# Numerators and denominators of a compressive memory in one product of 136 columns, copied by ScalarE, and an output that ends in halves

## The chip, the cores and the metric

The kernel runs on one core of one Trainium2 chip. The metric is the device time of one execution, in microseconds (us). The core has a matrix engine (TensorE, PE in the profile; its weight loads are PEld), three engines for elementwise work (VectorE or DVE, ScalarE or ACT, GpSimd or POOL), a queue for transfers (SyncE or SP) and two on-chip memories: SBUF, and the eight banks of PSUM that matmuls write.

## The reference

Two branches work on the same 2048 rows of 512 numbers, and a gate mixes them row by row: `out = g * a + (1 - g) * b`.

- `b` is a gated feed-forward layer of width 1792: `gelu(x @ w_gate) * (x @ w_up) @ w_down`.
- `a` is attention with 32 heads of 16 numbers, in 4 segments of 512 rows, with a memory that runs from segment to segment. What matters here:

```python
for s in range(N):
    p = softmax(qs @ ks.T * scale + mask)
    a_dot = p @ vs
    num = einsum('bhld,bhde->bhle', phi(qs), M)
    den = einsum('bhld,bhd->bhl', phi(qs), z)[..., None] + 1e-06
    o = gb * (num / den) + (1.0 - gb) * a_dot      # gb = sigmoid(beta), one per head
    M = M + einsum('bhld,bhle->bhde', phi(ks), vs)
    z = z + sum_l phi(ks)
a = concat(o) @ wo
```

Segment 0 has an empty memory, so the memory part is computed in segments 1 to 3. Inputs and outputs are bf16.

## The kernel before

**Tiles.** The 32 heads are four chunks `c` of eight heads, so there are 16 pairs (segment, chunk), numbered `i = 4*s + c`. A chunk's queries are 128 partitions (8 heads x 16) by 512 rows. Weights stay in SBUF all the time.

**Attention.** The kernel runs 72 visits. A visit computes a block of logits for four heads at a time into the only tile `lg` of four banks (`group_qk`, line 649, called QK below), ScalarE takes its exp into `pT` (line 654) and GpSimd masks the diagonal (line 658). When a chunk has all its eight blocks, two visits later a "lump" multiplies them with the values (`pv`, line 674, called PV below) into two banks `od`. VectorE transposes these (`oq`, line 681), divides by the softmax sums and scales (`norm`, lines 686 and 687, once for each of two halves), transposes the result into the chunk's part of `oT` (`back`, line 692), and adds the memory part `mT` (`add_mem`, line 695). These come 1, 2, 3 and 4 visits after the lump.

**Memory.** After each of the first three segments, `memory` (line 556) adds its products to `Macc`. `u_mask` makes two operands from it for the next segment: `Mn`, block-diagonal by heads with 128 columns a chunk, and `Mz` with 8 columns a chunk. `u_den` multiplies `phi(q)` (tile `pq`) with `Mz` (tile `zd`, line 599), and VectorE adds 1e-6, inverts and multiplies by the head's gate (`rdm`, lines 606, 609, 610), for two chunks at a time. `mem_num` multiplies `pq` with `Mn` into one bank `mn` (line 628); VectorE scales the bank by `rdm` into `tm` (line 632), and SyncE transposes `tm` into `mT` by a transfer (line 640). The scaling and the transfer are issued in `mem_num` itself.

**The other work.** Matmuls of all other parts (K, Q, V, gate, up, down, out) are units of 4 to 16 matmuls in streams: `gT` (line 473), `uT` (494), `dT` (510, 14 matmuls a unit) and `aT` (532, 4 a unit). They write the four banks of the pool `gen` in turn, which `mn`, `zd` and `od` use too. Their results are read out by VectorE, or by ScalarE where `cast` finds room (lines 309 and 313).

**The order.** All engines' instructions are put in order by a planner in the kernel's own Python. `t_pe` and `t_act` are its clocks for TensorE and ScalarE, `passed(pe, dve)` and `act(t)` advance them, `backlog` is VectorE's. Each visit issues QK, then a lump if one is due, then everything due in this visit (`later(n, f)` puts `f` into the n-th visit from now), then fills TensorE with units up to a `goal` at which the next QK may come; the numerator (`mem_num`) asked for at the end of the visit before is issued between two such fills. In the last segment the goal keeps 7.6 us of units (`TAIL_FILL`), and the last four `aT` units, for after the visits. There the last lump and all that is still due are issued:

```python
fill_to(t_pe[0] + TAIL_FILL * 0.42)
for f in pending:
    f()
for _, i in lumps:
    lump(i)
while due:
    for f in due.pop(min(due)):
        f()
fill_to(1e9)
```

`mem_num` of the last chunk runs in visit 72, the last. `left()` sums the units that have not begun. Each engine executes its instructions in the order of issue. `u_out` (lines 522 to 548) multiplies `oT` with `wo`, mixes with the other branch (line 538) and sends 128 rows out (line 547); the last 128 rows go in two halves.

Of the kernel before, what the change touches and what calls it, by code (L numbers as in the profile page):

```python
# [53 lines left out]
def kernel(  # L54
# [44 lines left out]
    gh = const([P, H], F32, "gh")  # L99
    og = const([P, H], F32, "og")  # L100
    Macc = const([P, NC8, 2, 17], F32, "Macc")
    Mn = [const([P, NC8, 128], BF, f"Mn{i}") for i in range(2)]
    Mz = [const([P, NC8, 8], BF, f"Mz{i}") for i in range(2)]
    rdm = [const([P, KT, H], F32, f"rdm{i}") for i in range(2)]
    ktb = const([P, NC8, L], BF, "ktb")
    pk = const([P, KT, D], BF, "pk")
    G = [const([P, HS, L], BF, f"G{i}") for i in range(NG)]
# [90 lines left out]
    def setup_consts():  # L198
        nc.gpsimd.memset(bm[:, :, :], 1.0)
        nc.gpsimd.affine_select(out=bm[:, :, :], in_=bm[:, :, :], pattern=[[-16, 8], [0, 17]],  # L200
                                compare_op=ALU.is_ge, fill=0.0, base=0, channel_multiplier=1)
        nc.gpsimd.affine_select(out=bm[:, :, :], in_=bm[:, :, :], pattern=[[16, 8], [0, 17]],
                                compare_op=ALU.is_ge, fill=0.0, base=15, channel_multiplier=-1)
        nc.vector.tensor_reduce(out=eo[:, 0:1], in_=bm[:, 0:8:2, 16],
                                axis=mybir.AxisListType.X, op=ALU.add)
        nc.vector.tensor_reduce(out=eo[:, 1:2], in_=bm[:, 1:8:2, 16],
                                axis=mybir.AxisListType.X, op=ALU.add)
        for i in range(2):
            ones = V[i][:, :, 0:2 * VE].rearrange("q k (h e) -> q k h e", h=H)[:, :, :, 16:18]
# [312 lines left out]
    def u_out(s, qt):  # L522
        def f():
            oT = oTs[s]
            q0 = s * L + qt * P
            tB = tBs[(s, qt // 2)]
            parts = 2 if (s, qt) == (NSEG - 1, KT - 1) and not general_now[0] else 1
            w = D // parts
            for d0 in range(0, D, w):
                T = gen("aT")  # L530
                for fc in range(FC):
                    nc.tensor.matmul(T[:, 0:w], lhsT=oT[:, fc, qt * P:(qt + 1) * P],  # L532
                                     rhs=wo[:, fc, d0:d0 + w],
                                     start=(fc == 0), stop=(fc == FC - 1))
                    if fc < FC - 1:
                        yield MM512 / parts
                osb = tB[:, qt % 2, d0:d0 + w]
                nc.vector.scalar_tensor_tensor(out=osb, in0=T[:, 0:w],  # L538
                                               scalar=gct[:, s, qt:qt + 1],
                                               in1=osb, op0=ALU.mult, op1=ALU.add)  # L540
                if s == 0 and qt == KT - 2:
                    continue
                if s == 0 and qt == KT - 1:
                    queue[0].dma_start(out2[q0 - P:q0 + P, :].rearrange("(k p) d -> p k d", p=P),
                                       tB[:, :, :])
                else:
                    queue[0].dma_start(out2[q0:q0 + P, d0:d0 + w], osb)
            return MM512
        return 4 * MM512, EVAC, f

# [16 lines left out]
    def u_mask(s):  # L567
        def half(h0):
            for c in (h0, h0 + 1):
                nc.vector.tensor_tensor(  # L570
                    out=Mn[s % 2][:, c, :].rearrange("q (j p d) -> q j p d", j=4, p=2),
                    in0=Macc[:, c, None, :, 0:16].to_broadcast((P, 4, 2, DH)),
                    in1=bm[:, :, 0:16].rearrange("q (j p) d -> q j p d", j=4), op=ALU.mult)
            passed(0.0, 0.6)
            done["Mn", s] = count(("Mn", s)) + 1

        def f():
            nc.vector.tensor_tensor(
                out=Mz[s % 2][:, :, :].rearrange("q c (j p) -> q c j p", j=4),
                in0=Macc[:, :, None, :, 16].to_broadcast((P, NC8, 4, 2)),  # L580
                in1=bm[:, None, :, 16].to_broadcast((P, NC8, 8))
                .rearrange("q c (j p) -> q c j p", j=4), op=ALU.mult)
            if general_now[0]:
                half(0)
                half(2)
            else:
                later(2, lambda: half(0))
                later(8, lambda: half(2))
        return 0.0, 0.2, f

    def u_den(s, pair):
        def f():
            assert general_now[0] or ("q", s, 2 * pair) in ready
            T = gen("zd")
            Tv = T[:, 0:KT * 16].rearrange("p (q h) -> p q h", q=KT)
            for cc in range(2):
                c = 2 * pair + cc
                for qq in range(KT):
                    nc.tensor.matmul(Tv[:, qq, 8 * cc:8 * cc + 8],
                                     lhsT=pq[:, c, qq * P:(qq + 1) * P],  # L600
                                     rhs=Mz[s % 2][:, c, :], start=True, stop=True)
                if cc == 0:
                    yield 0.12
            h0 = 16 * pair
            r = rdm[s % 2][:, :, h0:h0 + 16]
            nc.vector.tensor_scalar_add(r, Tv, 1e-6)

            def f_inv():
                nc.vector.reciprocal(r, r)
                nc.vector.tensor_tensor(out=r, in0=r,  # L610
                                        in1=gh[:, None, h0:h0 + 16].to_broadcast((P, KT, 16)),
                                        op=ALU.mult)
                passed(0.0, 0.8)
                done["inv", s] = count(("inv", s)) + 1
            if general_now[0]:
                f_inv()
            else:
                later(1, f_inv)
            return 0.12
        return 0.24, 0.22, f  # L620

    tms = {}

    def mem_num(s, c):
        assert general_now[0] or (count(("Mn", s)) > c // 2 and count(("inv", s)) > c // 2)
        T = gen("mn")
        for qq in range(KT):
            nc.tensor.matmul(T[:, qq * P:(qq + 1) * P],  # L628
                             lhsT=pq[:, c, qq * P:(qq + 1) * P], rhs=Mn[s % 2][:, c, :],
                             start=True, stop=True)  # L630
        tm = wk2.tile([P, KT, 8, DH], BF, name="tm", tag="tm")
        nc.vector.tensor_tensor(
            out=tm[:, :, :, :], in0=T[:, :].rearrange("p (q h d) -> p q h d", q=KT, h=8),
            in1=rdm[s % 2][:, :, 8 * c:8 * c + 8, None].to_broadcast((P, KT, 8, DH)), op=ALU.mult)
        mT = wk2.tile([P, L], BF, name="mT", tag="mT")
        mTv = mT[:, :].rearrange("p (q t) -> p q t", q=KT)
        if general_now[0]:
            turn(mTv, tm[:, :, :, :].rearrange("p q h d -> p q (h d)"))
        else:
            nc.sync.dma_start_transpose(mTv, tm[:, :, :, :].rearrange("p q h d -> p (q h d)"))  # L640
        tms[(s, c)] = mT

    def group_qk(pieces):
        lg = plg.tile([P, 4, 512], F32, name="lg", tag="lg")
# [236 lines left out]
    us = []  # L881
    for s in range(NSEG - 1):
        us.append(unit(u_mask(s + 1), 0, None, lambda s=s: count(("M", s)) == 1))
        us += [unit(u_den(s + 1, pair), NP * s + 16 + 9 * pair, ("den", s + 1),
                    lambda s=s, pair=pair: ("q", s + 1, 2 * pair) in ready)
               for pair in range(2)]
# [76 lines left out]

    def numerator(s, c):
        room_for_bank()
        mem_num(s, c)
        done["num", s] = count(("num", s)) + 1
        passed(0.3, EVAC)

    def can_num(s, c):  # L970
        if count(("den", s)) <= c // 2 and ("q", s, c - c % 2) in ready:
            need(("den", s), c // 2 + 1)
        return count(("Mn", s)) > c // 2 and count(("inv", s)) > c // 2

    asked = []
    pending = []
# [123 lines left out]
    def general():  # L1100
# [4 lines left out]
        for s in range(NSEG):  # L1105
# [16 lines left out]
            if s > 0:  # L1122
                for c in range(0, NC8, 2):
                    phi_now(pq[:, c:c + 2, :], QT[:, c:c + 2, :])
                run(u_mask(s))
                run(u_den(s, 0))
                run(u_den(s, 1))
# [75 lines left out]
```

## Time and profile before

| what | value |
|---|---|
| median of 3 runs (lowest to highest) | 268.8 us (268.23 to 269.04) |
| the profiled execution's own time | 268.51 us |
| its span in the profile | 266.8 us |
| busy TensorE / VectorE / ScalarE / GpSimd | 261.9 / 200.7 / 209.7 / 155.7 us |
| mean granted TensorE clock | 0.998 |

Rows of the profile name the line of the kernel, the engine, the tile written and the tiles read, and then a count (x8), the busy time and the mean of one instruction in ns, or, in a timeline, the start and the length in us. A releaser in brackets ends the idle time before an instruction. The chain that ended last follows the last instruction back, at each step to what released it.

### The profile page before, as it was taken

To read this page: it belongs to the slowest core of one execution; us is meant where nothing else is said; L and a number is where in the kernel's file an instruction comes from. 1 tells how busy PE (TensorE), PEld (TensorE's weight loads), DVE (VectorE), ACT (ScalarE), POOL (GpSimd) and SP (SyncE) were. 2 spreads that over 40 slices of the span, in tenths; PEclk is the share of its full clock that TensorE was granted. 3 is DMA by queue.
4 is the path that set the end of the run, shared out by engine and by line. 5 is a ranking of instruction groups with operands and counts; after the bars stand their busy time and mean duration, and the time that the engine had idled before them with its cause. 6 is when DMAs were issued, how large, how long until landed. Compare 5 with 4: busy or idle time off the path is not lost.

```text
span 266.8 us, 6876 instructions
## 1 busy us (share of the span) xinstructions
PE 261.9 (98%) x2861; PEld 117.1 (44%) x2861; DVE 200.7 (75%) x394; ACT 209.7 (79%) x164; POOL 155.7 (58%) x298
## 2 busy tenths in 40 slices
PE   7999999999999999999999999999999999999994
PEld 4454434344443444444445344444444444444442
DVE  2899574969569887698887858595978759698364
ACT  4236889988998899889999899889989997657510
POOL 3000158896716979678940899687694099654500
PEclk9999999999999999999999999999999999999999
DMA  6999941200222001300033010401000110003102
GB/s 210 343 168 277 308 121 39 42 4 1 61 64 42 2 0 42 79 6 20 2 61 84 0 23 20 64 20 22 20 23 23 45 22 12 10 20 42 41 22 84
DMA packets 30410, 16.60 MB, mean 62 GB/s; under 512 B 20008, under 2 KB 29096, under 8 KB 30376
## 3 DMA queue, kind: packets, MB, share of 16 engines
q1 hardware_dynamic: 30376, 16.14, 24.8%
q8 instruction: 23, 0.38, 0.6%
q14 instruction: 11, 0.09, 0.1%
HBM read 8.14 MB, written 2.10 MB: 38 GB/s over the span
## 4 chain that ended last, share of the span: by engine, by line
PE 94%; DVE 4%; issue 1%; DVEq 0%
PE dT L510 19%; PE uT L494 18%; PE gT L473 18%; PE lg L649 8%; PE od L674 7%; PE kT L376 5%; PE qT L290 5%; PE aT L532 5%; PE vT L414 4%; PE mn L628 1%; PE warm L166 1%; PE zT L430 1%; DVE G L500 1%; PE MT L556 1%; PE x0T L183 1%
## 5 line engine op out<-in xcount | busy, mean ns | idle before, releaser
L658 POOL TENSOR_SCALAR_AFFINE_SELECT pT<-pT 64x256 bf16<-64x256 bf16 x256 | 112.9, 441 | 94.1 <-ACT pT L654 81.3
L654 ACT ACTIVATE pT<-lg 128x2048 bf16<-128x2048 f32 x72 | 135.1, 1876 | 22.5 <-PE lg L649 21.6
L494 PE MATMUL uT<-x,wup 128*128 128x512 bf16 x224 | 60.6, 380 | 0.0
L473 PE MATMUL gT<-x,wga 128*128 128x512 bf16 x224 | 55.6, 380 | 0.0
L510 PE MATMUL dT<-wdn,G 128*128 128x512 bf16 x224 | 53.9, 380 | 0.0
L500 DVE TENSOR_TENSOR G<-uT,G 128x512 bf16<-128x512 f32 x56 | 38.1, 683 | 6.1 <-PE uT L494 5.9
L386 POOL TENSOR_SCALAR KTm<-ktb,eo 128x512 bf16<-128x512 bf16 x26 | 40.7, 1577 | 1.3
L681 DVE STREAM_TRANSPOSE oq<-od 128x512 f32<-128x512 f32 x32 | 21.0, 695 | 20.1 <-PE od L674 20.1
L473 PEld LDWEIGHTS <-wga 128*128 128x128 bf16 x224 | 20.7, 98 | 24.5 <-issue 2.4
L510 PEld LDWEIGHTS <-G 128*128 128x128 bf16 x224 | 20.4, 98 | 24.3 <-issue 2.8
L494 PEld LDWEIGHTS <-wup 128*128 128x128 bf16 x224 | 20.2, 97 | 24.5 <-issue 4.7
L649 PE MATMUL lg<-QT,KTm 32*128 32x192 bf16 (+7 forms) x512 | 28.6, 287 | 0.0
L313 DVE CAST G<-gT 128x512 bf16<-128x512 f32 x25 | 17.1, 686 | 5.8 <-PE gT L473 5.6
L649 PEld LDWEIGHTS <-KTm 32*128 32x128 bf16 x512 | 8.5, 92 | 29.5 <-issue 29.5
L674 PE MATMUL od<-pT,V 64*32 64x128 bf16 (+7 forms) x512 | 19.3, 284 | 0.0
L674 PE MATMUL od<-pT,Vs 64*32 64x128 bf16 (+7 forms) x512 | 18.9, 284 | 0.1
L488 ACT ACTIVATE G<-G 128x3584 bf16<-128x3584 bf16 x6 | 18.8, 3182 | 0.0
L687 DVE SCALAR_TENSOR_TENSOR o<-oq,ogs,rden 128x256 bf16<-128x256 f32 x32 | 17.1, 535 | 1.1
L376 PE MATMUL kT<-x,wk 128*128 128x512 bf16 x64 | 16.8, 383 | 0.4 <-DVE x L189 0.4
L290 PE MATMUL qT<-x,wq 128*128 128x512 bf16 x64 | 16.6, 379 | 0.0
L538 DVE SCALAR_TENSOR_TENSOR tB<-aT,gct,tB 128x512 bf16<-128x512 f32 (+1 forms) x17 | 11.9, 712 | 5.8 <-PE aT L532 5.5
L532 PE MATMUL aT<-wo,oT 128*128 128x512 bf16 (+1 forms) x68 | 16.2, 367 | 0.0
(96 smaller groups left out, 269.6 us busy)
## 6 DMA issues: line engine op xcount, KB each, us to landing
wup<-in_B_w_up_dram SPq DMA_DIRECT2D x1, 1792.0 KB, 10.4
wdn<-in_B_w_down_dram SPq DMA_DIRECT2D x1, 1792.0 KB
out_dram<-tB SPq DMA_DIRECT2D x13, 128.0 KB, 1.7
wga<-in_B_w_gate_dram SPq DMA_DIRECT2D x1, 1280.0 KB, 10.2
Vs<-V SPq DMA_DIRECT2D x8, 144.0 KB, 3.2
G<-in_A_x_dram SPq DMA_DIRECT2D x2, 256.0 KB, 2.8
wk<-in_A_wk_dram SPq DMA_DIRECT2D x2, 256.0 KB, 4.3
wq<-in_A_wq_dram SPq DMA_DIRECT2D x1, 512.0 KB, 5.7
```

The lines of the kernel that those rows point to most:

```text
L290: nc.tensor.matmul(T[:, :], lhsT=wq[:, fc, c * P:(c + 1) * P], rhs=xS[s % NX][:, fc, :], start=(fc == 0), stop=(fc == FC - 1))
L376: nc.tensor.matmul(T[:, :], lhsT=wk[:, fc, c * P:(c + 1) * P], rhs=xS[s % NX][:, fc, :], start=(fc == 0), stop=(fc == FC - 1))
L386: eng.tensor_scalar(out=KTm[:, (NC8 * s + c) % NK, :, p, :], in0=ktb[:, c, :].rearrange("q (b k) -> q b k", b=NB), scalar1=eo[:, p:p + 1], ...
L473: nc.tensor.matmul(T[:, :], lhsT=wga[:, fc, hs * P:(hs + 1) * P], rhs=xS[s % NX][:, fc, :], start=(fc == 0), stop=(fc == FC - 1))
L494: nc.tensor.matmul(T[:, :], lhsT=wup[:, fc, hs * P:(hs + 1) * P], rhs=xS[s % NX][:, fc, :], start=(fc == 0), stop=(fc == FC - 1))
L500: nc.vector.tensor_tensor(out=g, in0=T[:, :], in1=g, op=ALU.mult)
L510: nc.tensor.matmul(T[:, :], lhsT=G[s % NG][:, hs, qt * P:(qt + 1) * P], rhs=wdn[:, hs, :], start=(hs == 0), stop=(hs == HS - 1))
L532: nc.tensor.matmul(T[:, 0:w], lhsT=oT[:, fc, qt * P:(qt + 1) * P], rhs=wo[:, fc, d0:d0 + w], start=(fc == 0), stop=(fc == FC - 1))
L649: nc.tensor.matmul(lg[:, j, off:off + n], lhsT=KTm[rows, i % NK, b].rearrange("r p k -> r (p k)"), rhs=QT[rows, i % NC8, 64 * b:L], start= ...
L654: nc.scalar.activation(pT[:, :, :], lg[:, :, :], AF.Exp, scale=DH ** -0.5)
L658: nc.gpsimd.affine_select(out=v, in_=v, pattern=[[0, 4], [1, 64]], compare_op=ALU.is_ge, fill=0.0, base=0, channel_multiplier=-1)
L674: nc.tensor.matmul(od[p][32 * j:32 * j + 32, 64 * b:L], lhsT=w[:, 18 * h:18 * h + 32], rhs=t[rows, j, off:off + n], start=(b == 0), stop=( ...
```

## The change

Numerator and denominator come out of one product. `Mn` has 136 columns a chunk, the last 8 of which take the place of `Mz`; the stream units `u_den` go. `mem_num` takes two banks of 272 columns (two blocks of 128 rows each); ScalarE copies each to an f32 tile `raw` in SBUF; the inversion (three VectorE instructions for one chunk) is due one visit later, and the scaling and the transposing transfer two visits later. The planner books 0.9 us on ScalarE for the copies and fills TensorE up to shortly before the end of the visit's exp ahead of the numerator.

The end: the last 256 rows, instead of the last 128, are computed in halves of 256 columns. The rows before the last 128 are still sent in one transfer; the first half of the last rows is sent from ScalarE's queue. At the start, two small reductions become one.

```diff
-    Mn = [const([P, NC8, 128], BF, f"Mn{i}") for i in range(2)]
-    Mz = [const([P, NC8, 8], BF, f"Mz{i}") for i in range(2)]
-    rdm = [const([P, KT, H], F32, f"rdm{i}") for i in range(2)]
+    Mn = [const([P, NC8, 136], BF, f"Mn{i}") for i in range(2)]
...
-        nc.vector.tensor_reduce(out=eo[:, 0:1], in_=bm[:, 0:8:2, 16],
-                                axis=mybir.AxisListType.X, op=ALU.add)
-        nc.vector.tensor_reduce(out=eo[:, 1:2], in_=bm[:, 1:8:2, 16],
+        nc.vector.tensor_reduce(out=eo[:, :],
+                                in_=bm[:, :, 16].rearrange("q (j p) -> q p j", p=2),
                                 axis=mybir.AxisListType.X, op=ALU.add)
...
-            parts = 2 if (s, qt) == (NSEG - 1, KT - 1) and not general_now[0] else 1
+            final = s == NSEG - 1 and not general_now[0]
+            parts = 2 if final and qt >= KT - 2 else 1
...
+                elif final and qt == KT - 2:
+                    if d0 > 0:
+                        queue[0].dma_start(out2[q0:q0 + P, :], tB[:, qt % 2, :])
                 else:
-                    queue[0].dma_start(out2[q0:q0 + P, d0:d0 + w], osb)
+                    q = nc.scalar if final and qt == KT - 1 and d0 == 0 else queue[0]
+                    q.dma_start(out2[q0:q0 + P, d0:d0 + w], osb)
...
-    def u_den(s, pair):
...
     def mem_num(s, c):
+        assert general_now[0] or count(("Mn", s)) > c // 2
+        raw = wk2.tile([P, KT, 136], F32, name="raw", tag="raw", bufs=1)
+        for h in range(2):
+            T = gen("mn")
+            for k in range(2):
+                qq = 2 * h + k
+                nc.tensor.matmul(T[:, 136 * k:136 * k + 136], lhsT=pq[:, c, qq * P:(qq + 1) * P],
+                                 rhs=Mn[s % 2][:, c, :], start=True, stop=True)
+            nc.scalar.copy(raw[:, 2 * h:2 * h + 2, :].rearrange("p k e -> p (k e)"),
+                           T[:, 0:272])
+        rd = wk2.tile([P, KT, 8], F32, name="rd", tag="rd")
+
+        def f_inv():
+            nc.vector.tensor_scalar_add(rd[:, :, :], raw[:, :, 128:136], 1e-6)
+            nc.vector.reciprocal(rd[:, :, :], rd[:, :, :])
+            nc.vector.tensor_tensor(out=rd[:, :, :], in0=rd[:, :, :],
+                                    in1=gh[:, None, 8 * c:8 * c + 8].to_broadcast((P, KT, 8)),
+                                    op=ALU.mult)
+            passed(0.0, 0.3)
+
+        def f_scale():
+            tm = wk2.tile([P, KT, 8, DH], BF, name="tm", tag="tm")
+            nc.vector.tensor_tensor(
+                out=tm[:, :, :, :], in0=raw[:, :, 0:128].rearrange("p q (h d) -> p q h d", h=8),
+                in1=rd[:, :, :, None].to_broadcast((P, KT, 8, DH)), op=ALU.mult)
+            passed(0.0, 0.65)
+            mT = wk2.tile([P, L], BF, name="mT", tag="mT")
...
+                nc.sync.dma_start_transpose(mTv, tm[:, :, :, :].rearrange("p q h d -> p (q h d)"))
+            tms[(s, c)] = mT
...
+        else:
+            act(0.9)
+            later(1, f_inv)
+            later(2, f_scale)
...
     def numerator(s, c):
         room_for_bank()
+        room_for_bank()
         mem_num(s, c)
         done["num", s] = count(("num", s)) + 1
-        passed(0.3, EVAC)
+        passed(0.3)
 
     def can_num(s, c):
-        if count(("den", s)) <= c // 2 and ("q", s, c - c % 2) in ready:
-            need(("den", s), c // 2 + 1)
-        return count(("Mn", s)) > c // 2 and count(("inv", s)) > c // 2
+        return count(("Mn", s)) > c // 2 and ("q", s, c - c % 2) in ready
...
-    act_left[0] = len(visits) * EXP_T + 3 * (GELU_T + 4 * PHI_T)
+    act_left[0] = len(visits) * EXP_T + 3 * (GELU_T + 4 * PHI_T) + 12 * 0.9
...
         fill_to(t_pe[0] + 0.5 * (goal - t_pe[0]))
+        if pending:
+            fill_to(min(goal - 0.3, t_act[0] - 0.3))
         for f in pending:
             f()
```

More of the change, by code (lines that the diff above doesn't have):

```diff
@@ L570, in half @@
                 nc.vector.tensor_tensor(
-                    out=Mn[s % 2][:, c, :].rearrange("q (j p d) -> q j p d", j=4, p=2),
+                    out=Mn[s % 2][:, c, 0:128].rearrange("q (j p d) -> q j p d", j=4, p=2),
                     in0=Macc[:, c, None, :, 0:16].to_broadcast((P, 4, 2, DH)),
@@ L578, in f @@
             nc.vector.tensor_tensor(
-                out=Mz[s % 2][:, :, :].rearrange("q c (j p) -> q c j p", j=4),
+                out=Mn[s % 2][:, :, 128:136].rearrange("q c (j p) -> q c j p", j=4),
                 in0=Macc[:, :, None, :, 16].to_broadcast((P, NC8, 4, 2)),
@@ L589, in u_mask @@
         return 0.0, 0.2, f
-    def u_den(s, pair):
[L592 to L620, printed above, removed]
@@ L622 @@
     tms = {}
     def mem_num(s, c):
[L625 to L634, printed above, removed]
@@ L635, in mem_num @@
-        mT = wk2.tile([P, L], BF, name="mT", tag="mT")
-        mTv = mT[:, :].rearrange("p (q t) -> p q t", q=KT)
+        assert general_now[0] or count(("Mn", s)) > c // 2
[8 more added lines that the diff above has]
+                           T[:, 0:272])
@@ new lines, in mem_num @@
+        rd = wk2.tile([P, KT, 8], F32, name="rd", tag="rd")
[13 more added lines that the diff above has]
+            mT = wk2.tile([P, L], BF, name="mT", tag="mT")
+            mTv = mT[:, :].rearrange("p (q t) -> p q t", q=KT)
+            if general_now[0]:
+                turn(mTv, tm[:, :, :, :].rearrange("p q h d -> p q (h d)"))
+            else:
+                nc.sync.dma_start_transpose(mTv, tm[:, :, :, :].rearrange("p q h d -> p (q h d)"))
+            tms[(s, c)] = mT
@@ L637, in mem_num @@
         if general_now[0]:
-            turn(mTv, tm[:, :, :, :].rearrange("p q h d -> p q (h d)"))
-        else:
-            nc.sync.dma_start_transpose(mTv, tm[:, :, :, :].rearrange("p q h d -> p (q h d)"))
-        tms[(s, c)] = mT
+            f_inv()
+            f_scale()
+        else:
+            act(0.9)
+            later(1, f_inv)
+            later(2, f_scale)
     def group_qk(pieces):
@@ L883 @@
         us.append(unit(u_mask(s + 1), 0, None, lambda s=s: count(("M", s)) == 1))
-        us += [unit(u_den(s + 1, pair), NP * s + 16 + 9 * pair, ("den", s + 1),
-                    lambda s=s, pair=pair: ("q", s + 1, 2 * pair) in ready)
-               for pair in range(2)]
     streams.append(Stream("M", us))
@@ L1125, in general @@
                 run(u_mask(s))
-                run(u_den(s, 0))
-                run(u_den(s, 1))
             neg = G[(s + 1) % NG][:, 8, 0:P]
```

## The prediction, made before the changed kernel ran

> **What bounds the kernel now.** I read the page first, then the chain that ended last from 247 us on, then the timelines of VectorE, SyncE and TensorE in that stretch, then the groups by form and the waits. The page, parts 1, 2 and 4:
>
> ```profile
> PE 261.9 (98%) x2861; PEld 117.1 (44%) x2861; DVE 200.7 (75%) x394; ACT 209.7 (79%) x164; POOL 155.7 (58%) x298
> ...
> PE   7999999999999999999999999999999999999994
> ...
> PE 94%; DVE 4%; issue 1%; DVEq 0%
> ```
>
> TensorE is busy in every slice but the first and the last, and the chain is 94% TensorE. So a matmul taken out comes off the time, work of the other engines counts only where it makes TensorE wait, and the one place to look at closely is the last slice. The chain there (start, length, what):
>
> ```profile
> 247.98 0.54 PE aT L532 x2
> ...
> 251.77 0.86 PE aT L532 x4
> 252.63 1.51 PE dT L510 x7
> 254.14 1.10 PE od L674 x64
> 255.24 4.64 PE dT L510 x21
> 259.88 2.60 PE aT L532 x12
> ```
>
> After the last PV product (L674) the 21 matmuls of dT cover the time in which VectorE turns that product into oT. The rows of VectorE, and of the weight loads, that end this cover:
>
> ```profile
> 255.36 1.31 DVE L681 STREAM_TRANSPOSE oq<-od 128x512 f32<-128x512 f32 x2 [1.87 <-PE od L674]
> 256.60 0.67 DVE L692 STREAM_TRANSPOSE oT<-o 128x512 bf16<-128x512 bf16 x1
> 257.19 0.21 DVE L686 RECIPROCAL rden<-oq 128x16 f32<-128x16 f32 x1
> 257.44 0.48 DVE L687 SCALAR_TENSOR_TENSOR o<-oq,ogs,rden 128x256 bf16<-128x256 f32 x1
> 257.84 0.42 DVE L695 TENSOR_TENSOR oT<-oT,mT 128x512 bf16<-128x512 bf16 x1
> ...
> 258.97 0.71 DVE L692 STREAM_TRANSPOSE oT<-o 128x512 bf16<-128x512 bf16 x1
> 259.72 0.42 DVE L695 TENSOR_TENSOR oT<-oT,mT 128x512 bf16<-128x512 bf16 x1
> ...
> 260.20 0.70 PEld L532 LDWEIGHTS <-oT 128*128 128x128 bf16 x4 [0.16 <-DVE oT L695]
> ```
>
> The last addition of the memory part ends at 260.14, and the weight load that wants it has been waiting 0.16 us. The cover has no slack: whatever makes that addition later makes the end later, one for one.
>
> **Matmuls removed and added.** TensorE's timeline between 234 and 242 us:
>
> ```profile
> 236.47 0.34 PE L599 MATMUL zd<-Mz,pq 128*128 128x8 bf16 x8
> ...
> 237.07 1.90 PE L494 MATMUL uT<-x,wup 128*128 128x512 bf16 x8
> ...
> 241.41 0.39 PE L628 MATMUL mn<-Mn,pq 128*128 128x128 bf16 x4
> ```
>
> One zd lasts 0.166 and one mn 0.219 (groups by form), so a step is (0.34-0.166)/7 = 0.025 us for 8 columns, (0.39-0.219)/3 = 0.057 for 128 and (1.90-0.38)/7 = 0.217 for 512. The 48 zd go: 48 x 0.025 = 1.2. The 48 mn grow by 8 columns at (0.217-0.057)/384 = 0.0004 each: 48 x 0.0033 = 0.16. TensorE: **-1.0 us**, all on the chain.
>
> **The memory step in the visits (12 chunks).** Added on ScalarE: 24 copies of 272 columns from a bank to f32. No row has this size; 4 columns take 0.199 (L447) and 512 take 0.594 (L309), so about 0.41 each, 0.83 a chunk, 9.9 in all. On VectorE, the inversion was 0.214+0.525+0.309 six times and becomes twelve times about 0.8 with its gaps: 0.17 for an addition of 32 numbers (L218), 0.35 for a reciprocal of 32 (L219), 0.25 for the product (between 0.212 of L578 and 0.309 of L610). That is some 3 us more, on an engine that is 75% busy. The scaling moves from a bank to f32 in SBUF. Its bounds are 0.427 (bf16 addition in SBUF, L695) and 0.681 (the scaling itself, L632); I take 0.68, the nearer in type. [...] No row here has f32 from SBUF at this size.
>
> What hides this: the copies queue on ScalarE behind the exp of their visit and ahead of the next exp, so they delay that exp, its masks on GpSimd and the next QK, which waits for the single logits tile. The trace has an exp start some 0.45 after its QK begins (QK at 239.77, exp at 240.22), and the QK itself a little after the exp before it, so most of the 0.83 fills a gap that is idle now; 0.2 to 0.4 per chunk is left. The slack to take it from:
>
> ```profile
> ACT pT L654 <- PE lg L649: 21.6, 43, 1.4
> ```
>
> 43 waits of at least 0.45 are 19.4 us, so 2 us are true surplus, and 44 evacuations on ScalarE (L309, 26.7 us) can go to VectorE. TensorE fills the visits with other work; I take +0.2 for QKs that come a little early (bounds 0 and 1.2, 0.1 for each of 12), and nothing for banks, since the two banks are read within 0.9 us and two others turn meanwhile. SyncE's transpose of tm moves two visits back with its place in the program, so nothing new stands behind it. The single reduction at the start and the wider Mn cost nothing that TensorE sees.
>
> **The memory step of the last chunk.** Before, it is early:
>
> ```profile
> 249.86 0.69 DVE L632 TENSOR_TENSOR tm<-mn,rdm 128x512 bf16<-128x512 f32 x1 [0.55 <-PE mn L628]
> ...
> 250.58 1.20 SPq L640 DMA_TRANSPOSE mT<-tm  x1
> ```
>
> After, its product is still in visit 72, but the inversion is due in 73 and the scaling in 74. Those are issued after the last PV, and VectorE is in order: both stand behind the two oq transposes at 255.36, though their input is ready by about 251. In order of issue: oq, oq, oT of chunk 2, inversion (0.8), first norm (0.65, from 257.19 to 257.84), addition of chunk 2 (0.33), scaling (0.68). On before's clock the scaling ends at 257.19+0.80+0.65+0.33+0.68 = 259.65. The transpose is issued 0.03 later (as 250.55 to 250.58) and lands 2.4 later (the median of its 12, part 6): 262.08. Second norm and oT transpose end at 261.2, so the DMA is what comes last. The addition ends at 262.08+0.05+0.42 = 262.55 instead of 260.14: **2.4 later**, with TensorE standing still if its cover is the same 21 matmuls.
>
> The cover is not fixed. The planner leaves about 7.6 us plus whatever is left of the unit in progress at the last QK (0.43 before: the two matmuls of aT at 247.98) and spends 3.2 before the PV. If a dT unit of 14 is in progress, up to 2.8 more is left; if less than 0.43, 0.4 less. I count 0.4 more cover, as most of the work there is dT: **+2.0** (bounds 0 and 2.8).
>
> **The end in halves.** Evacuations of 512 step by 0.67 and of 256 by 0.39 (262.57 to 263.24; two in 0.87). With chunk 2 in halves the last starts at 261.72+0.67+3x0.39 = 263.56 instead of 263.63. The last output transfer, now 0.14 after its evacuation behind another on SyncE (others: 0.03), loses that wait since one goes to ScalarE's queue: together **-0.2** (bounds -0.2 and +0.2; no row has a transfer issued by ScalarE).
>
> **Sum.** -1.0+0.2+2.0-0.2 = +1.0 us. The profiled execution took 268.5 (span 266.8), so 269.5; it lies 0.3 below the median of the runs, 268.8, so against that **269.8**. A measurement of this kernel can tell some 0.3% (0.8 us) from no change: below 268.0 is faster, above 269.6 slower.
>
> **Rivals.** (a) The planner leaves more dT after the last PV. For it: 42 of the 48 matmuls of dT and aT between the last QK and the last PV's cover are dT (the chain), in units of 14. Against: which unit is open at the last QK can't be read from this trace. It decides from 32 matmuls (21 plus 2.4/0.217): the tail then costs nothing, and -1.0-0.2+0.2 gives 267.8. With 27 to 31 it is 268.0 to 268.9. (b) ScalarE becomes the bound: the copies delay each of the next exps by 0.4, 12 x 0.4 = 4.8 less the surplus of 2.3, so 2.5 us in which TensorE has no fill left at the last visits, and 269.8+2.5 = 272.3, or 271 if half is covered. For it: ScalarE is 90% busy from 95 to 200 us (94.8 of 105, the table by stretches). Against: the exps from 230 to 245 us wait 0.6 to 1.4 for QK (ScalarE's timeline), so late in the kernel ScalarE has room. It decides once copies and casts together exceed the gaps before QK. (c) The tail as costed, 21 to 26 matmuls of cover: 269.1 to 270.2.
>
> **Chances.** (c) 0.57, of which 0.12 lies within 0.3%; (a) with full cover 0.13, with part of it 0.15; (b) 0.15. So faster 0.13, same 0.15+0.12 = 0.27, slower 0.45+0.15 = 0.60. The range leaves out most of (a) with full cover below and the far end of (b) above: 268.0 to 271.6.
>
> **What would show it.** No zd rows; mn steps of 0.060; ACT copies of 0.41 in pairs before an exp; the last tm scaling behind the oq transposes, its DMA some 2.4 us before the last addition, and a weight load of aT that waits 1 to 2.6 us for DVE oT. Wrong if that wait is under 0.3 with the scaling in this place (a), or if QK's matmuls wait for ACT in many visits (b).

## The result and the profile after

The changed kernel takes 281.79 us (median of 6 runs, 280.99 to 282.77), the kernel before 268.52 beside it (6 runs, 268.23 to 269.04): 1.0507 times as long, interval 1.0489 to 1.0525. That is 13.3 us slower, where +1.0 was forecast and 271.6 was the upper end of the range. The profiled execution took 282.63 us with a span of 280.9, so 14.1 more than the span of before.

The page of the changed kernel, parts 1, 2 and 4: busy time by engine, busy tenths of TensorE in 40 slices of 7.0 us, its granted clock in the same slices, and the chain that ended last.

```profile
PE 264.8 (94%) x2817; PEld 118.6 (42%) x2817; DVE 210.8 (75%) x421; ACT 211.1 (75%) x179; POOL 160.4 (57%) x298
...
PE   6999999999999999999939999999989998999984
...
PEclk9999999999999999999977999999999999999999
...
PE 77%; DVE 12%; ACT 4%; issue 3%; DMA 2%; SPq 0%; DVEq 0%
```

Before, TensorE was full in every slice but the first and the last, and the chain was 94% TensorE. Now there is a hole in slice 21, with the clock at 0.7 there and in the slice after it, and 8 instead of 9 in slices 30 and 34 (from 204 and from 232 us) and in slice 39 (from 267 us), the tail. VectorE is 10 us busier, ScalarE only 1.4: its 24 copies took room that the planner then kept free of evacuations (35 on ScalarE instead of 44, 71 on VectorE instead of 62).

TensorE's own waits, by the line that waited and what it waited for (us in total, times, longest). Before, the view had two entries, both in the first 6 us:

```profile
PE warm L166 <- PEq L1187: 1.0, 1, 1.0
PE kT L376 <- DVE x L189: 0.4, 1, 0.4
```

Of the changed kernel:

```profile
PE dT L507 <- DVE G L497: 5.2, 1, 5.2
PE aT L530 <- DVE oT L689: 1.8, 1, 1.8
PE kT L373 <- DMA wk<-in_A_wk_dram: 1.5, 1, 1.5
PE mn L602 <- DVE tB L312: 1.0, 1, 1.0
...
PE mn L602 <- DVE G L497: 0.6, 1, 0.6
PE uT L491 <- DVE tB L536: 0.5, 1, 0.5
PE od L668 <- DVE G L497: 0.5, 1, 0.5
PE mn L602 <- DVE tB L536: 0.3, 1, 0.3
PE od L668 <- DVE G L310: 0.2, 1, 0.2
```

Three kinds of loss stand here. One stall of 5.2 us in mid-kernel; one of 1.8 at the end, the tail that was forecast; and six waits of 0.2 to 1.0 us, 3.1 in all, three of them at the second pair of a numerator's product, each on a VectorE instruction that reads a bank out. (The wait for a weight transfer at the start, 1.1 longer than the one before, costs next to nothing: the first qT starts at 8.90 us, before at 8.85. e2, e4 and e6 have such a wait too, of 0.6 to 1.3.)

**The stall.** TensorE's timeline (start, length, what, and in brackets the idle time and its releaser) around it, and four kT at full clock to compare with:

```profile
137.00 2.97 PE L507 MATMUL dT<-wdn,G 128*128 128x512 bf16 x13
145.18 0.61 PE L507 MATMUL dT<-wdn,G 128*128 128x512 bf16 x1 [5.21 <-DVE G L497]
...
147.07 1.91 PE L373 MATMUL kT<-x,wk 128*128 128x512 bf16 x4
...
199.66 1.03 PE L373 MATMUL kT<-x,wk 128*128 128x512 bf16 x4
```

The last of 14 dT wants the last slice of `G`, the product of uT and the gate (L497). VectorE's timeline says why that came late:

```profile
143.72 0.18 DVE L609 TENSOR_SCALAR rd<-raw 128x32 f32<-128x32 f32 x1 [4.75 <-ACT raw L604]
...
144.44 0.68 DVE L497 TENSOR_TENSOR G<-uT,G 128x512 bf16<-128x512 f32 x1
```

VectorE stood idle for 4.75 us in front of the inversion (L609), with the read-out of uT behind it in its queue. The inversion waited for ScalarE's copies, and ScalarE's timeline shows what stood ahead of them:

```profile
135.57 1.28 ACT L485 ACT_TABLE_LOAD   x1
136.87 6.27 ACT L485 ACTIVATE G<-G 128x3584 bf16<-128x3584 bf16 x2
143.04 0.65 ACT L604 COPY raw<-mn 128x272 f32<-128x272 f32 x2
143.71 1.28 ACT L648 ACT_TABLE_LOAD   x1
145.00 1.88 ACT L648 ACTIVATE pT<-lg 128x2048 bf16<-128x2048 f32 x1
```

The GELU of segment 2 (L485), a table load and 6.27 us, was issued in the same visit as the numerator and ahead of it. The numerator's product had run at 135.47, so its second copy ended 8.2 us later. Before, that GELU came one visit after the numerator, behind another QK and its exp, and the numerator's bank, which VectorE read at 133.52, could not stand behind it:

```profile
132.74 0.39 PE L628 MATMUL mn<-Mn,pq 128*128 128x128 bf16 x4
133.92 0.39 PE L649 MATMUL lg<-QT,KTm 32*128 32x512 bf16 x4
134.37 1.88 ACT L654 ACTIVATE pT<-lg 128x2048 bf16<-128x2048 f32 x1
136.26 1.28 ACT L488 ACT_TABLE_LOAD   x1
137.56 6.27 ACT L488 ACTIVATE G<-G 128x3584 bf16<-128x3584 bf16 x2
```

The stall is paid twice. For 5.3 us behind it, up to 150.5, the granted clock is 0.5 and a step of 512 columns takes (1.91-0.63)/3 = 0.427 us instead of (1.03-0.38)/3 = 0.217 (0.63 and 0.38 are one kT, by the groups by form): 2.7 us lost. Together some 8 us.

**The tail.** The chain that ended last, in order of time (start, length, what):

```profile
268.01 0.68 DVE oq L675
268.68 0.59 DVE oT L686
...
270.15 0.49 DVE o L681
270.64 0.33 DVE oT L689
270.97 0.60 DVE tm L618
...
271.60 2.41 DMA mT<-tm
...
274.11 0.44 DVE oT L689
...
274.59 1.70 PE aT L530 x9
```

The inversion and the scaling of the last chunk stand behind the oq transposes, the transfer lands 2.41 later, and the weight load of aT waits for the last addition. From the start of the last addition to the end of the span it is 6.8 us, before 7.1.

### The profile page after: what moved, and what is told of

It is laid out like the page before. It is cut to its first block, busy times and chain, and to the rows that moved or that the text cites. A ratio compares the mean times of both kernels' runs of the same rounds, so it can differ in the third digit from the quotient of the medians.

```text
span 280.9 us, 6832 instructions
## 1 busy us (share of the span) xinstructions
PE 264.8 (94%) x2817; PEld 118.6 (42%) x2817; DVE 210.8 (75%) x421; ACT 211.1 (75%) x179; POOL 160.4 (57%) x298
## 4 chain that ended last, share of the span: by engine, by line
PE 77%; DVE 12%; ACT 4%; issue 3%; DMA 2%; SPq 0%; DVEq 0%
PE gT L470 16%; PE uT L491 14%; PE dT L507 13%; PE lg L643 7%; PE od L668 6%; PE qT L287 5%; PE kT L373 5%; PE vT L411 4%; PE aT L530 4%; ACT G L485 2%; DVE G L497 2%; DVE oq L675 2%; DMA wk<-in_A_wk_dram 2%; DVE o L681 1%; ACT pT L648 1%
## 5 line engine op out<-in xcount | busy, mean ns | idle before, releaser
L652 POOL TENSOR_SCALAR_AFFINE_SELECT pT<-pT 64x256 bf16<-64x256 bf16 x256 | 118.0, 461 | 99.2 <-ACT pT L648 86.9
L491 PE MATMUL uT<-x,wup 128*128 128x512 bf16 x224 | 58.9, 380 | 0.5 <-DVE tB L536 0.5
L497 DVE TENSOR_TENSOR G<-uT,G 128x512 bf16<-128x512 f32 x56 | 37.6, 682 | 5.3 <-PE uT L491 5.0
L310 DVE CAST G<-gT 128x512 bf16<-128x512 f32 x29 | 19.9, 686 | 5.9 <-PE gT L470 5.6
L643 PEld LDWEIGHTS <-KTm 32*128 32x128 bf16 x512 | 9.4, 92 | 26.4 <-issue 25.1
L485 ACT ACTIVATE G<-G 128x3584 bf16<-128x3584 bf16 x6 | 18.8, 3182 | 0.0
```

The costliest lines, as they stand in the source:

```text
L491: nc.tensor.matmul(T[:, :], lhsT=wup[:, fc, hs * P:(hs + 1) * P], rhs=xS[s % NX][:, fc, :], start=(fc == 0), stop=(fc == FC - 1))
L497: nc.vector.tensor_tensor(out=g, in0=T[:, :], in1=g, op=ALU.mult)
L643: nc.tensor.matmul(lg[:, j, off:off + n], lhsT=KTm[rows, i % NK, b].rearrange("r p k -> r (p k)"), rhs=QT[rows, i % NC8, 64 * b:L], start= ...
L652: nc.gpsimd.affine_select(out=v, in_=v, pattern=[[0, 4], [1, 64]], compare_op=ALU.is_ge, fill=0.0, base=0, channel_multiplier=-1)
```

## The experiments

Each was run in rounds beside the kernel before; "above before" is the difference of the two medians. e1 to e6 and e8 edit the changed kernel, e7 and e9 to e12 the kernel before. Line numbers in their profiles shift by the lines added.

**e1: the GELU one visit later whenever a numerator is about to be issued.**

```diff
             def g():
+                if pending:
+                    later(1, g)
+                    return
                 gelu(s)
```

> The changed kernel, with one edit to the order: a GELU that is due in a visit in which a numerator is pending is issued one visit later, so that the copies of that numerator stand ahead of it on ScalarE. All work is kept. Theory 1 (order): in the changed kernel the two copies of one chunk stand behind a GELU of 7.6 us (135.6 to 143.0 us), VectorE's inversion waits for them and everything behind it on VectorE too, TensorE stands still for 5.4 us, and its granted clock is halved for the next 5 us, which costs some 2.5 more. Then this edit takes off about 8 us: 274 us, with a mean clock of 0.998 again. Theory 2 (load): ScalarE has 8 to 10 us more work than it has room for, and the time is lost wherever that shows first. Then the stall moves and the time stays above 279.

Measured: 274.6 us, 6.3 above before, ratio 1.0229 (1.0210 to 1.0247). 7.0 of the 13.3 are gone, by order alone, with the work unchanged. (The rest of the order moves with it: the third GELU starts at 201.2 us, in the changed kernel at 213.9.) ScalarE's timeline of this run:

```profile
135.50 0.67 ACT L604 COPY raw<-mn 128x272 f32<-128x272 f32 x2
136.04 1.91 ACT L648 ACTIVATE pT<-lg 128x2048 bf16<-128x2048 f32 x1
137.97 1.28 ACT L485 ACT_TABLE_LOAD   x1
139.26 6.27 ACT L485 ACTIVATE G<-G 128x3584 bf16<-128x3584 bf16 x2
```

The copies now run ahead of an exp and the GELU. TensorE's dT waits 0.3 us for VectorE in all, and the clock stays at 1.0.

**e2: inversion and scaling two visits later, the GELU left ahead of the copies** (the last chunk as in the changed kernel).

```diff
-            later(1, f_inv)
-            later(2, f_scale)
+            n = 0 if (s, c) == (NSEG - 1, NC8 - 1) else 2
+            later(1 + n, f_inv)
+            later(2 + n, f_scale)
```

> The changed kernel, with the inversion due 3 instead of 1 and the scaling 4 instead of 2 visits after the numerator, but for the last chunk, which stays as it is. All work is kept; the copies of one chunk still stand behind a GELU. If TensorE's stall of 5.4 us comes from VectorE standing in line behind the inversion (whose input ScalarE makes late), the stall goes, although two of the four banks are held for 7.6 us: 273 to 275 us. If it comes from the two banks that are held, it stays, and so does the time, above 279. VectorE's other waits for the copies (4.6 of 9.4 us in the changed kernel) should go under both theories, and with them some of the 4.2 us in which TensorE waits for banks at 201 to 251 us.

Measured: 277.0 us, 8.7 above before, ratio 1.0316 (1.0297 to 1.0335). The profiled execution took 280.68 us, the others 276.91 to 277.06; its mean granted clock was 0.994 and theirs 0.999 to 1.0, which over its span of 278.8 us makes 1.4 to 1.7 of the difference. TensorE's longest waits there:

```profile
PE mn L602 <- DVE tB L536: 1.9, 1, 1.9
PE mn L602 <- DVE G L497: 1.5, 2, 1.0
```

The stall of dT is gone, and no inversion waits for a copy. So it was the inversion standing in VectorE's queue that carried ScalarE's delay to TensorE. ScalarE still holds the two banks for the length of a GELU here (137.4 to 144.9 us), and the one wait of TensorE for such a copy is 0.25 us. The gain is smaller than expected: in this execution the waits at the numerator's banks are 3.4 us, in the changed kernel 1.9.

**e3: the last chunk's inversion and scaling issued with its product.**

```diff
+            if (s, c) == (NSEG - 1, NC8 - 1):
+                f_inv()
+                f_scale()
+                return
             act(0.9)
```

> The changed kernel, with the inversion, the scaling and the transposing transfer of the last chunk alone issued in the visit of its numerator. All work is kept. If TensorE's stall of 2.0 us before the last weight load of aT comes from the transfer, which lands late because the scaling stands behind the oq transposes on VectorE, this takes off 2.0 us: 279.8 us, with the wait for oT under 0.3. If the addition were late for another reason (more VectorE work in all), less than 0.5 comes off.

Measured: 280.45 us, 12.1 above before, so 1.1 less than the changed kernel; ratio 1.0452 (1.0429 to 1.0476). The end of its chain has no VectorE and no transfer left between the last PV and the outputs:

```profile
265.24 1.10 PE od L672 x64
...
266.50 4.70 PE dT L507 x21
271.20 2.18 PE aT L530 x12
```

The tail is the place and the mechanism that was forecast. The stall of dT is there as in the changed kernel (5.2).

**e5: e1 and e3 together.**

```diff
+            if (s, c) == (NSEG - 1, NC8 - 1):
+                f_inv()
+                f_scale()
+                return
...
+                if pending:
+                    later(1, g)
+                    return
```

> The two edits to the order together: the GELU behind the copies of a pending numerator, and the last chunk's inversion, scaling and transfer in the visit of its numerator. Alone they came to 274.6 us, and to 2 us less TensorE standing still. If the two losses are independent, this is 274.6 - 2.0 = 272.6 us, still 4 above the kernel before; what is left would be TensorE's waits for banks (3.8 us of them in the profile of the first edit, at 168 to 243 us) less the 1.0 us of matmuls saved.

Measured: 272.82 us, 4.4 above before, ratio 1.0164 (1.0149 to 1.0178), and 1.9 less than e1. So order costs about 9 us, and 4.4 are left. Where they are, TensorE's timeline shows:

```profile
168.20 0.28 PE L602 MATMUL mn<-Mn,pq 128*128 128x136 bf16 x2
169.79 0.28 PE L602 MATMUL mn<-Mn,pq 128*128 128x136 bf16 x2 [1.31 <-DVE G L497]
...
242.38 0.28 PE L602 MATMUL mn<-Mn,pq 128*128 128x136 bf16 x2
243.30 0.28 PE L602 MATMUL mn<-Mn,pq 128*128 128x136 bf16 x2 [0.64 <-DVE G L497]
```

The first pair of products has its bank, and the second pair waits until VectorE has read out an older one: 1.47 and 0.80 us (from the start of one matmul to the start of the next, less the step of a matmul). With 0.94 and 0.42 before a uT and a dT near 205 us and 0.68 before a uT at 236.8, five gaps sum to 4.3 (the dT may have waited for `G` itself and not for a bank). Less the 1.0 that the matmuls save, that is 3.3 of the 3.9 us by which this span (270.7) exceeds that of before; where the rest lies was not traced.

**e4: no ScalarE; VectorE adds, inverts and scales from the two banks at once.**

```diff
-            nc.scalar.copy(raw[:, 2 * h:2 * h + 2, :].rearrange("p k e -> p (k e)"),
-                           T[:, 0:272])
+            Ts.append(T[:, 0:272].rearrange("p (k e) -> p k e", k=2))
+        for h in range(2):
+            nc.vector.tensor_scalar_add(rd[:, 2 * h:2 * h + 2, :], Ts[h][:, :, 128:136], 1e-6)
...
+        for h in range(2):
             nc.vector.tensor_tensor(
...
-            act(0.9)
-            later(1, f_inv)
-            later(2, f_scale)
```

> One product of 136 columns in two banks a chunk, but without ScalarE: VectorE adds, inverts and scales from the banks in the visit of the numerator, and the transfer is issued there, as in the kernel before. The planner books 1.9 us on VectorE for it and nothing on ScalarE. The end in halves is kept. If the loss is the detour over ScalarE and the two visits that it puts between product and transfer, this is at or below the kernel before: 267 to 269 us, since TensorE keeps the 1.0 us of matmuls that went. If two banks at once are themselves the trouble, TensorE waits at the second pair of a numerator here too (2.5 us or more in the changed kernel), and the time is 270 to 273.

Measured: 272.55 us, 4.2 above before, ratio 1.0151 (1.0130 to 1.0171). Without any copy, and with no tail, it costs about the same as e5. So what is left does not need ScalarE's copies; what e4 and e5 share against before is the product in two banks and more work on VectorE (205.9 and 210.2 us busy, before 200.7). The wait that was expected at the second pair of a numerator did not come: TensorE waits some 3 us for VectorE here too, but only 0.4 of it at mn, the rest at od, dT and uT.

**e6: e5 with one bank in each of two successive visits.**

```diff
+        mem_num(s, c, (0,))
+        carry.append(lambda: second(s, c))
+    def second(s, c):
+        mem_num(s, c, (1,))
```

> Both edits to the order, and each numerator in two visits: its first bank one visit earlier, its second where it was, each with room made for one bank. Copies, inversion and scaling are the same work. If the rest of the loss comes from taking two banks at once (the second pair of a numerator waits for a bank that VectorE has not read yet: 1.45 and 0.80 us in the first edit's profile), those waits go: 270.0 to 270.7 us. If it comes from VectorE having 9 us more to do, so that any bank is read late, waits of the same sum appear elsewhere: 272 to 273.

Measured: 278.58 us, 10.1 above before, ratio 1.0383 (1.0368 to 1.0398). The new order put a PV behind the transfer of its values (`Vs`) for 3.7 us, and the mean granted clock of the profiled execution was 0.994, which over its span of 276.3 us is another 1.7. Without these two, 4.7 of the 10.1 are left, about what e5 lost, though no numerator's product waits for a bank any more: uT, od and others wait 3.2 us for VectorE in its place. That is the second of the two expectations, but the order differs in too much to decide it.

**e8: e5 with VectorE's part booked in full in the planner** (0.9 for the inversion, 0.85 for the scaling), where the changed kernel books 0.3 and 0.65.

```diff
-            passed(0.0, 0.3)
+            passed(0.0, 0.9)
...
-            passed(0.0, 0.65)
+            passed(0.0, 0.85)
```

> Both edits to the order, and the planner books on VectorE what the change really costs there: 0.9 us for the inversion instead of 0.3, and 0.85 for the scaling instead of 0.65 (the rows of the changed kernel: 0.30+0.35+0.21 and 0.77). The work is the same, the order is the planner's. If the waits for banks come from a planner that thinks VectorE freer than it is, this is 1 to 2 us below the kernel with both edits to the order alone (271 to 271.5); if the waits come from two banks at once whatever the booking, it stays within 0.7 us of it.

Measured: 272.52 us, ratio 1.0147 (1.0133 to 1.0162), 0.3 under e5. What the planner thinks of VectorE isn't it.

**e7: the kernel before with the new end alone** (5 rounds).

```diff
-            parts = 2 if (s, qt) == (NSEG - 1, KT - 1) and not general_now[0] else 1
+            final = s == NSEG - 1 and not general_now[0]
+            parts = 2 if final and qt >= KT - 2 else 1
...
+                elif final and qt == KT - 2:
+                    if d0 > 0:
+                        queue[0].dma_start(out2[q0:q0 + P, :], tB[:, qt % 2, :])
```

> The kernel before, with only the end changed: the last 256 rows in halves, and the first half of the last rows sent from ScalarE's queue. By the prediction's term the end comes 0.2 us earlier (0.07 on VectorE, 0.11 of waiting on SyncE's queue): a ratio of 0.9992, within what can just be told. If the first transfer of ScalarE's queue costs more than the wait that it saves, the ratio is 1.000 to 1.001.

Measured: 268.39 against 268.45 us, ratio 1.0002 (0.9982 to 1.0022). A gain of 0.2 can neither be seen nor excluded.

The last four take the kernel before and add one part each of what e5 still has.

**e9: booked for the copies without having them**, so that only the order changes, and with it which engine reads a bank out: 71 evacuations on VectorE and 35 on ScalarE, as in the changed kernel. (With it a reduction of the input came due in a visit already begun; it is put one visit later.)

```diff
-                later(periods[fc] - clock[0], g)
+                later(max(1, periods[fc] - clock[0]), g)
...
+        act(0.9)
...
-    act_left[0] = len(visits) * EXP_T + 3 * (GELU_T + 4 * PHI_T)
+    act_left[0] = len(visits) * EXP_T + 3 * (GELU_T + 4 * PHI_T) + 12 * 0.9
```

> The kernel before, all of its work and none of the change's, but with the planner booking 0.9 us of ScalarE for each numerator (act and act_left as in the change). So only the order of the units, the choice of the reading engine and the place of the visits move. What is left of the loss once the GELU and the last chunk are put right is 4.4 us. If that is the price of another order (the order of before happens to make TensorE wait for nothing, and another one waits), this is 270 to 273 us with waits of TensorE for banks. If it is the work that the change adds, this is within 0.8 us of the kernel before.

Measured: 269.75 us, 1.4 above before, ratio 1.0055 (1.0036 to 1.0073): less than a change of order as the whole cause would give, more than none. VectorE is 5.1 us busier than before, yet TensorE waits for it or for GpSimd only 0.4 us in all behind the start; what makes this kernel longer, its trace does not show.

**e10: 24 copies of 272 columns on ScalarE whose results nothing uses**, two with each numerator.

```diff
+        nc.scalar.copy(idle1[:, :], idle0[:, :])
+        nc.scalar.copy(idle1[:, :], idle0[:, :])
```

> The kernel before in its own order, with two copies of 272 f32 columns within SBUF added on ScalarE after each numerator (24 in all, some 9 us; their result isn't used), and the planner not told. If ScalarE has no room for 9 us, exps come later, TensorE waits at QK, and this is 2 us or more slower than before; if the copies fit the gaps ahead of the exps, as the prediction had it, less than 0.8 us.

Measured: 270.07 us, 1.8 above before, ratio 1.0056 (1.0040 to 1.0073). ScalarE's load has a price, of this size: TensorE's QK waits for an exp three times, 1.0 us in all.

**e11: 24 additions of 272 columns on VectorE whose results nothing uses**, one and two visits after each numerator.

```diff
+        later(1, lambda: nc.vector.tensor_scalar_add(idle1[:, :], idle0[:, :], 1.0))
+        later(2, lambda: nc.vector.tensor_scalar_add(idle1[:, :], idle0[:, :], 1.0))
```

> The kernel before in its own order, with two additions to 272 f32 columns within SBUF on VectorE, one and two visits after each numerator (24 in all, 7 to 10 us, about what VectorE has more in the changed kernel; their result isn't used), and the planner not told. If VectorE's load is what makes TensorE wait for banks, this is 2 to 4 us slower than before; if VectorE has room, less than 0.8 us.

Measured: 269.74 us, 1.4 above before, ratio 1.0062 (1.0028 to 1.0095). So more work on VectorE has a price too. TensorE waits 0.7 and 0.4 us for read-outs in this trace, and two of the additions (0.4 us) stand in the chain of the end, behind the last oq; that these are the whole price is not shown.

**e12: the numerator in two banks of 256 columns**, each scaled by VectorE; order and planner as before. (So the planner makes room for one bank and the numerator takes two; the changed kernel makes room for two.)

```diff
+        Ts = [gen("mn") for h in range(2)]
...
-            nc.tensor.matmul(T[:, qq * P:(qq + 1) * P],
+            nc.tensor.matmul(Ts[qq // 2][:, qq % 2 * P:(qq % 2 + 1) * P],
```

> The kernel before in its own order, with each numerator in two banks of 256 columns instead of one of 512, and VectorE scaling each by itself (0.3 us more on VectorE a chunk). No work for ScalarE, no other plan. Booking the copies alone cost 1.5 us, 9 us on ScalarE alone 1.5, 7 us on VectorE alone 1.6; these three less the 1.0 of matmuls saved make 3.6 of the 4.4 us that stay when both orders are put right. If two banks at once have a price of their own, it is the rest, about 0.8 us, and this kernel is 0.8 to 1.5 us slower than before, with a wait of TensorE at the second pair of mn. If not, it is within 0.5 us of it.

Measured: 271.24 us, 3.0 above before, ratio 1.0108 (1.0091 to 1.0125), twice what was expected and the largest price of the four. TensorE's timeline has a loss of this kind right behind a numerator:

```profile
166.49 0.39 PE L629 MATMUL mn<-Mn,pq 128*128 128x128 bf16 x4
166.72 0.38 PE L473 MATMUL gT<-x,wga 128*128 128x512 bf16 x1
168.41 0.59 PE L510 MATMUL dT<-wdn,G 128*128 128x512 bf16 x2 [1.31 <-DVE V L313]
```

Here the numerator got both of its banks, and the unit behind it waits 1.31 for one. At another numerator (226.4 us) the second bank comes 0.56 late. The price holds more than the bank: VectorE scales 24 times 0.41 us instead of 12 times 0.68 (0.8 more), and no room was made for the second bank. The four prices sum to 1.4+1.8+1.4+3.0 = 7.6, more than the 4.4 of e5 with the 1.0 that the matmuls save, 5.4: they overlap and can't be added up. How much of the rest each holds stays open. e12 says that a second bank can cost most; e4 and e6 say that a like loss comes with hardly a wait at the numerator's own product.

None of the twelve was measurably faster than the kernel before.

## Why the prediction was wrong, step by step

**The matmuls: right.** No zd is left, and four mn take 0.40 us in a row with 0.222 for one, a step of (0.40-0.222)/3 = 0.059 where 0.060 was expected. The terms of 1.2 and 0.16 stand, though what they save is lost at the banks.

**The tail: right in place, order and size.** It was costed at +2.0. The groups by form (count, busy us, mean ns, idle before) give the pieces:

```profile
L604 ACT COPY raw<-mn 128x272 f32<-128x272 f32 x24 | 8.3, 392 | 1.3 <-PE mn L602 1.3
L609 DVE TENSOR_SCALAR rd<-raw 128x32 f32<-128x32 f32 x12 | 3.6, 299 | 9.5 <-ACT raw L604 9.4
L618 DVE TENSOR_TENSOR tm<-raw,rd 128x512 bf16<-128x512 f32 x12 | 9.3, 773 | 0.0
```

A copy took 0.39 (0.41 estimated). The last scaling took 0.69 in VectorE's timeline (0.68 taken, the upper of its two bounds), and its transfer landed 2.41 later (2.4). The cover was 22 dT, within the 21 to 26 of the case (c), and TensorE stood still for 2.0 us (2.22 between two starts, less a step of 0.22). e3 took 1.1 off and e5, against e1, 1.9. Rival (a), more cover, did not come: 22 matmuls were left after the last PV, and 32 were needed.

**The end in halves, -0.2: open.** e7 can't tell it from nothing; the 6.8 instead of 7.1 us behind the last addition agree with it.

**The visits, +0.2 with bounds 0 and 1.2: wrong, and nearly the whole error.** The stall with the clock behind it (7.9) and the waits for banks (3.1) stand where 0.2 was put. Two statements of that step failed.

"the copies queue on ScalarE behind the exp of their visit and ahead of the next exp". That looked at the exps and not at what else ScalarE executes. Three times it has a GELU, 7.6 us with its table load, and a visit in which GELU and numerator meet puts the copies behind that. The wait which the change adds was followed on ScalarE, for the next exp; it was not followed on the engine that reads the copies, where the inversion, one visit later, holds up every read-out behind it. The group above has 9.4 us in which rd waits for raw. The 4.75 of them in the visit of the GELU, with the inversion and the read-out that followed, became TensorE's 5.2, and then 2.7 of half clock. e1 took 7.0 off by order alone. The upper bound of 1.2 was twelve times 0.1 for a QK that comes a little early, and no term of it held a late read-out.

"nothing for banks, since the two banks are read within 0.9 us and two others turn meanwhile". A pair of copies takes 0.65 to 0.68 us once it runs; but from the start of the first product to the end of the second copy it is 1.0 to 2.0 us in eleven chunks, and 8.2 in the one behind the GELU. Nor are the banks before them in the ring free sooner. TensorE can use a second bank at once only if the unit that had it has been read out; in the two pairs shown above it had not been, by VectorE, which is now 10 us busier. Of these, 6.5 are the nine evacuations that moved over from ScalarE (48.4 us in the groups by form, before 41.9): the prediction counted on that move as slack and put no price on it. In e5 such waits cost some 4.3 us at five places; in the kernel before, TensorE had no such wait at all, which says that nothing waited, not how little slack there was. How the loss divides between the second bank (3.0 in e12, with what else that run changes) and VectorE's later read-outs stays open.

**Rival (b), ScalarE as the bound: no.** It named the right engine and the wrong mechanism: exps late, QK waiting. No QK appears among TensorE's waits of the changed kernel; in e10, where no evacuation moves over, it does, for 1.0 us. The load of the copies was worth 1.8 us (e10), their place in the queue 7.0.

## What to carry to other kernels

A step moved to an in-order engine inherits the longest instruction that can stand ahead of it there, and passes that on to the engine where its consumer waits in line (here 7.6 us of GELU, 4.75 of VectorE standing idle, 5.2 of TensorE); so look at every instruction of the new engine, and at what is queued behind the consumer. A trace without waits for buffers does not say how much slack the buffers have: before asking for two where one was asked for, price the next user of the ring. When a stall of TensorE is priced, look at the granted clock behind it too: here it added half as much again (2.7 us to 5.2).

## What the runs showed of the hardware

**The granted clock fell behind a stall, and not alike in all executions.** In the profiled execution of the changed kernel no matmul ran from 139.97 to 145.18 us. The granted clock was 0.67 on average from 143 to 145, with 1.00 up to 143.5 and 0.50 from 144, so it fell at 143.7, 3.7 us behind the last matmul; it was 0.50 from 145 to 150, and back at full from 150.5. The stretch at half clock lasted 6.8 us, and the mean clock of this execution was 0.987. Of the kernel's other five executions three had a mean of 0.986 to 0.988 and two of 0.994. e3, with a stall of 5.2 us, had 0.988 in all four; e6, with a wait of 3.7, had 0.985, 0.988 and twice 0.994; e2, whose longest wait was 1.9, had 0.994 in the profiled execution and 0.999 to 1.0 in the four others. In e5 and e12, with waits of up to 1.31, the mean of the profiled execution was 1.0, and the 2.0 us of standing still in the tail of the changed kernel left the clock at 1.00 (264 to 279 us). How long TensorE has to stand still for the clock to fall, these numbers do not show.

**The scaling from SBUF took longer in six of twelve executions, each begun beside a mask of GpSimd.** Its 12 executions took 0.65 to 0.69 us six times and 0.80 to 0.90 six times; from the bank, before, it was 0.67 to 0.69 in all. The six from 0.80 up each began while a mask of GpSimd (L652) was running, with 0.27 to 0.36 us of that mask to come. Of the other six, two have no GpSimd work beside them (0.68 and 0.69), two began 0.02 us ahead of a mask (0.65 both), and two began when the GpSimd instruction in progress had 0.07 and 0.18 us to come (0.68 both). The masks that began after a scaling, while it ran, took 0.74 to 0.91 us, where the median of all masks is 0.41. What makes the one or the other longer, the trace does not show.
